# Three moves in the order of work: a difference of y, one gated product, and the differences of w_out

## The chip, the cores and the metric

The kernel runs on one core of one Trainium2 chip. The metric is the device time of one execution in microseconds (us), the median of three runs. PE is the matrix engine, DVE the vector engine, ACT the scalar engine, POOL the GpSimd engine and SP the engine whose queue issues most DMAs. PSUM is the memory that PE writes its products to, SBUF the memory for everything else on the core.

## The reference

Two blocks follow one another. The first is a chunked state space scan (batch 4, 8 heads, 768 positions, head size 32, state size 16); its output `y` becomes a matrix of 3072 tokens by 256. The second is a feed-forward block:

```
h = x @ w_in            # 3072x256 @ 256x2048
g = h * np.cos(h)
return (g @ w_out)      # 3072x2048 @ 2048x256
```

The arrays `w_in` and `w_out` come as 64-bit floats; the kernel makes 32-bit floats of them on the core.

## The kernel before

**Steps.** The tokens are worked in six chunks (`NC = 6`, counted from 0) of 512: 128 positions of four sequences. A chunk has 16 steps (`NF = 16`); step `n` is step `f` of chunk `c`, with `c, f = divmod(n, 16)`. A step takes half a chunk (256 tokens, `u`) and two of the sixteen 128-wide tiles of the hidden size (the pair `j` of eight). It has these parts:

- `first(n)` (line 660): eight PE instructions give `hp`, 128 by 512 values in PSUM. Steps in a "run" (`sevens`: steps 9 to 13 of chunks 2, 3 and 4, and 13 of the last chunk's steps) use `first7` (line 760) instead. It makes the same block from seven smaller products, with differences of `w_in` (`wid`, made once by `differ_in`) and differences of `y` (`yd`, made for each chunk by `differ_y`, line 742, the tile called `m` in the profile). Its products are issued in the order 1, 6, 7, 5, 4, 3, 2; product 4 reads the fourth difference `d[:, 3]`.
- `wind_k` (ACT, line 667), `wind_w` (DVE, line 673) and `gate` (ACT, line 682) give the cosine of `hp`.
- `gated(n)` (DVE, line 687) multiplies: `gT = hp * cos`. It is the last reader of `hp[n]`, so it frees the PSUM bank that a later `first` writes; outside the runs two such banks take turns from step 4 on, so `first(n)` waits for `gated(n - 2)`. For steps of chunk 1 and later, `gated` also calls `differ(n)`, three POOL instructions (lines 712, 714, 715, tile `gd`).
- `second(n)`, issued two steps later (`LAG = 2`): in chunk 0 eight PE instructions (line 796) with rows of `w_out`; from chunk 1 on `seven(n)`, fourteen PE instructions (line 836) that read `gT`, `gd`, `w_out` and the differences of `w_out` (`wd`, in the profile the tile `words`).

**Weights.** Each weight matrix comes in eight pieces. `grade` takes a piece apart: ACT makes the absolute value of the high word (line 248) and scales the low word (line 246), POOL clamps (line 249). `join(which, i)` puts it together: a DVE shift and mask (line 261), a DVE combination with the sign (line 263) and a POOL add (line 271) that writes the finished piece. `piece` says which piece is joined in which step: step `n` joins piece `n // 2` of `w_out` if `n` is even, a piece of `w_in` if it is odd. Step 4 joins piece 2 of `w_out`, the piece that the second products of steps 4 and 5 read.

**Differences of w_out.** `differ_w(i, js)` (POOL, line 706) makes difference `i` of four for a range of pairs: `fore` is four pairs, `mid` two, `hind` two. `differ_at` says after which step. The first reader is `seven(16)`, issued in iteration 18; `mid` is read first by `seven(20)`, in iteration 22.

**Order.** The schedule is written by hand: an engine executes its instructions in the order in which the program issues them, and waits by semaphores. Steps 0 to 3 stand in `first_steps`; the loop starts at step `AHEAD = 4`. In an iteration the loop issues `first(n)`, `wind_k`, `wind_w`, the next `grade`, `gate`, the `join`, `gated(n)`, then work of the scan (`decays0`, a DVE scan `lam`, line 375, and `weigh0`, POOL line 381), then `differ_y`, the sums of finished outputs (POOL line 861), `differ_w`, and last `second(n - 2)`. `differ_y` is called in steps 4 to 7 of chunks 2, 3 and 4, one difference a step, on POOL, for the second half of the chunk. Difference 3 reads difference 2.

Of the kernel before, what the change touches and what calls it, by code (L numbers as in the profile page):

```python
# [25 lines left out]
def kernel(  # L26
# [13 lines left out]
    V, ACT, G, PE = nc.vector, nc.scalar, nc.gpsimd, nc.tensor  # L40
# [4 lines left out]
    NC = S // P  # L45
    DM, DF = moe_w_in.shape
    KT = DM // P
    NF = DF // P
# [204 lines left out]
        if later:  # L253
            return rest

    def join(which, i):


        parts = held.pop((which, i), ())
        for e, (high, bits, last) in enumerate(parts):  # L260
            V.tensor_scalar(out=bits, in0=bits, scalar1=3, scalar2=0x3FFFFFFF,  # L261
                            op0=ALU.logical_shift_left, op1=ALU.bitwise_and)
            V.scalar_tensor_tensor(out=bits, in0=high, scalar=0xC0000000, in1=bits,
                                   op0=ALU.bitwise_and, op1=ALU.bitwise_or)
            dst = kept(which, i)
            if len(parts) > 1:
                dst = dst[:, :, e * P:(e + 1) * P]
            else:
                bits, last = (ap.rearrange("p (k f) -> p k f", k=dst.shape[1])
                              for ap in (bits, last))  # L270
            G.tensor_tensor(out=dst.bitcast(U32), in0=bits, in1=last, op=ALU.add)
# [412 lines left out]
    def gated(n):  # L684
        cos = turns.pop(n)
        gT[n] = ffn.tile([P, TB], FP32, tag="gT", bufs=LAG + 1, name="gT")
        V.tensor_tensor(out=gT[n], in0=hp.pop(n), in1=cos, op=ALU.mult)  # L687
        gT[n] = gT[n].rearrange("p (q m) -> p q m", q=4)
        if NF <= n < NC * NF - 1:
            differ(n)  # L690
# [42 lines left out]
    def differ_y(c, i, eng, us=slice(0, 2)):  # L733

        if i == 0:
            yd[c] = ms[2].rearrange("p (i u m) -> p i u m", i=4, u=2)
        d = yd[c]
        y11, y12, y21, y22 = (yT[c][:, us, k, h * P:(h + 1) * P] for k in range(2)
                              for h in range(2))
        a_ = (y12, y22, y22, y21)[i]  # L740
        b_ = (y11, y12, d[:, 0, us], d[:, 2, us])[i]
        eng.tensor_tensor(out=d[:, i, us], in0=a_, in1=b_,  # L742
                          op=ALU.add if i in (1, 2) else ALU.subtract)
# [203 lines left out]
    def store_a(dst, src):  # L947
# [3 lines left out]

    piece = {n: ("in", (n + 3) // 2) if n % 2 else ("out", n // 2) for n in range(NF)}
    fore, mid, hind = slice(0, NJ // 2), slice(NJ // 2, 3 * NJ // 4), slice(3 * NJ // 4, NJ)
    differ_at = {NF - 2: [(0, fore), (1, fore)], NF - 1: [(2, fore), (3, fore)],
                 **{NF + i: [(i, mid)] for i in range(4)},
                 NF + 4: [(0, hind)], NF + 5: [(1, hind)], NF + 6: [(2, hind), (3, hind)]}


# [61 lines left out]
    AHEAD = 4  # L1020
# [83 lines left out]
    for n in range(AHEAD, NC * NF + LAG):  # L1104
        c, f = divmod(n, NF)
        if n < NC * NF:

            if c > 0 and f in (loads_of := (6, 7, 8, 9) if c == 1 else (0, 1, 2, 3)):
                load(c + 2, loads_of.index(f))
            if n in (NF - 4, NF - 3):  # L1110
                load_arow(n - NF + 8)
            if n == NF - 2:
                for k in (4, 5):
                    for s in range(2):
                        load_x(k, s)
            if n in (NF - 1, NF):
                load_along(2, (2 * (n == NF), 2 * (n == NF) + 1))
            for e, i in chunks_at(n, "along"):
                load_along(e + 1, (2 * i, 2 * i + 1))
            if n in sevens or n - 1 in sevens:  # L1120
                first_of_seven(n)
            else:
                first(n)
            if n not in sevens and n - 1 in sevens:
                wind(n - 1)
                gate(n - 1)
                gated(late.pop())
            closing = f == NF - 1 and 1 <= c < NC - 1
            take_y = finish2(c + 1) if closing else None
            if n not in sevens:  # L1130
                wind_k(n)
                wind_w(n)
            if closing:
                take_y(0)
            for e, s in chunks_at(n - 1, "turn"):
                turn2(e, s)
            for k in units_at(n, 2):
                turn_unit(k)
            if n + 1 in piece:
                rests_of.append(grade(*piece[n + 1], later=True))  # L1140
            if n not in sevens:
                gate(n)
            while len(rests_of) > (n == AHEAD):
                rest = rests_of.pop(0)
                if rest:
                    rest()
            joins = n in piece and piece[n] in held
            if joins:
                join(*piece[n])

            behind = [lambda at=at: decays2(*at) for at in decays_at(n)]
            behind += [lambda k=2 * c - 1 + i: add_state(k) for c, i in chunks_at(n, "state")]
            behind += [lambda c=c, b=2 * s + p: reaches(c, b) for c, s in chunks_at(n, "reach")
                       for p in range(2)]
            behind += [lambda at=at: turn_blocks(*at) for at in chunks_at(n, "turn")]
            behind += [lambda k=k, p=p: decays0(k, p) for k, at in unit_at.items()
                       for p in range(2) if at[0][p] == n]
            behind = [lambda k=2 * c + i, q=q: weights(k, q) for c, i in chunks_at(n, "weigh")
                      for q in range(2)] + behind
            behind = [lambda k=k: weights(k, 1) for k in units_at(n - 1, 3)] + behind  # L1160
            if not joins and behind:
                behind.pop(0)()
            if n + 1 in sevens or n in sevens:
                late.append(n)
            else:
                gated(n)
            if closing:
                take_y(1)
            if n == NF + 7:
                weigh0(5)  # L1170
            if add_s and (n == NF - 5 or units_at(n - 1, 4)):
                exchange = add_s()
                add_s = None
            if n == NF + 9:
                exchange()
            for do in behind:
                do()
            if n == runs[-1][0] - 2:
                for i in range(4):
                    differ_y(NC - 1, i, V)  # L1180
            if 2 <= c < NC - 1 and 4 <= f <= 7:
                differ_y(c, f - 4, G, slice(1, 2))
            if unsummed and (c > 1 or summed[0]):
                unsummed[0](range(summed[0], summed[0] + 1), G)
                summed[0] = (summed[0] + 1) % 4
                if summed[0] == 0:
                    unsummed.pop()
            elif n not in sevens and f not in ((10, 11, 12) if c == 1 else (10, 11)):
                for do in unsummed:
                    do()  # L1190
                unsummed.clear()
            for k, ((_, last_), *_) in unit_at.items():
                if last_ == n:
                    weigh0(k)
        for i, js in differ_at.get(n, ()):
            differ_w(i, js)
        for start, js in zip((2 * NF - 5, 3 * NF - 3, 4 * NF - 3),
                             (slice(1, 6), slice(0, 1), slice(6, NJ))):
            if start <= n < start + 4:
                differ_in(n - start, js)  # L1200
        if f == NF - 2 and 1 < c < NC - 1:
            open2(c + 1)
        if n == AHEAD + 1:
            second(AHEAD - LAG)
        if n >= LAG and n != AHEAD:
            second(n - LAG)
        for e, _ in chunks_at(n, "inner"):
            inner2(e)
        for k in units_at(n, 3):
            for t in range(2):  # L1210
                inner(k, t)
            if k == 3:
                at = [gs[k, s][:, 0, 2 * P:] for s in range(2)]
                sums(4, at, group)
                take_sums((4,), at)
            weights(k, 0)
        for k in units_at(n, 4):
            take_s, add_s = finish0(k)
            take_s()
        for k in units_at(n, 1):  # L1220
            reach_unit(k)
        if n == 2 * NF - 3:
            open2(2)
        for at, e in block_loads.items():
            if at == n:
                loading = load_blocks(e)
            if at <= n < at + 12:
                next(loading)
# [30 lines left out]
```

## Time and profile before

| what | value |
|---|---|
| median of 3 runs | 366.38 us (366.14 to 366.74) |
| the profiled execution | 365.9 us, of which the span from first to last instruction is 364.1 us |
| granted clock of PE | 0.999 |
| PE busy | 356.6 us, 98% of the span |
| DVE busy | 275.6 us, 76% |
| POOL busy | 238.5 us, 65% |
| ACT busy | 183.9 us, 51% |

A row of the timeline gives the start, the time from start to end, the engine, the line, the operation, what is written from what, shapes, and the number of merged instructions; a bracket tells the idle time before and what ended it. A busy PE can hide a wait, since ends of matmuls are modelled; the distance between the starts of like rows shows it. Instructions overlap a little: on DVE the next one starts some 0.08 us before the end of the one before.

### The profile page before, as it was taken

Reading aid. Unit: us, or ns where it says so; the run is one execution under the profiler, and the core shown is the slowest. Engines: PE = TensorE matmul, PEld = TensorE weight load, DVE = VectorE, ACT = ScalarE, POOL = GpSimd, SP = SyncE. Lnnn points to the kernel's source line nnn. Section 1 sums busy time; section 2 is a strip of 40 time slices with the busy share of each in tenths; the row PEclk is TensorE's granted clock in tenths of the full one; section 3 lists DMA queues with packets and bytes.
Section 4 is the critical chain, followed back from the end, with each engine's and each line's share of the span. In section 5 each row is a group of like instructions: output and inputs, shape, how many; then the busy total and the mean of one; then the engine's idle time right before and its main releaser. Section 6 shows DMA issues by size and latency. Waiting matters only on the chain.

```text
span 364.1 us, 10279 instructions
## 1 busy us (share of the span) xinstructions
PE 356.6 (98%) x4070; PEld 326.1 (90%) x4070; DVE 275.6 (76%) x504; ACT 183.9 (51%) x352; POOL 238.5 (65%) x387
## 2 busy tenths in 40 slices
PE   7999999999999999999999999999999999999995
PEld 4788888888999999999989998999999999999995
DVE  7789998588777977877766877775776775778774
ACT  3597766544455254634445543545453544454542
POOL 5567757579866885765775666686666565475562
PEclk9999999999999999999999999999999999999999
DMA  7996957692564447011328102110001001001001
GB/s 140 274 358 136 214 109 119 109 135 58 112 105 71 91 93 104 8 44 41 75 58 122 17 6 66 31 34 12 0 2 31 0 3 32 0 3 31 1 15 46
DMA packets 97328, 26.43 MB, mean 73 GB/s; under 512 B 87328, under 2 KB 93184, under 8 KB 97280
## 3 DMA queue, kind: packets, MB, share of 16 engines
q1 hardware_dynamic: 96032, 25.38, 34.0%
q8 instruction: 32, 0.52, 0.6%
q10 hardware_dynamic: 1248, 0.39, 0.5%
q14 instruction: 16, 0.13, 0.1%
HBM read 22.36 MB, written 3.34 MB: 71 GB/s over the span
## 4 chain that ended last, share of the span: by engine, by line
PE 80%; DVE 6%; POOL 5%; SPq 2%; issue 2%; ACT 2%; DMA 2%; POOLq 0%; ACTq 0%; DVEq 0%
PE o L836 30%; PE hp L660 25%; PE m L760 7%; PE hp L760 5%; PE o L796 5%; PE y L629 2%; POOL gd L712 1%; DMA bc<-in_B_dram 1%; DVE w L673 1%; POOL gd L714 1%; DVE mag L261 1%; PE y L477 1%; POOL m L742 1%; ACT k L667 1%; PE y L617 1%
## 5 line engine op out<-in xcount | busy, mean ns | idle before, releaser
L660 PE MATMUL hp<-yT,w_in 128*128 128x256 f32 x544 | 129.4, 382 | 0.3 <-DVE gT L687 0.3
L660 PEld LDWEIGHTS hp<-yT,w_in 128*128 128x128 f32 x544 | 99.1, 190 | 13.6 <-issue 1.0
L712 POOL TENSOR_TENSOR gd<-gT 128x256 f32<-128x256 f32 x79 | 59.8, 757 | 77.6 <-DVE gT L687 64.0
L682 ACT ACTIVATE w<-w,quarter 128x512 f32<-128x512 f32 x96 | 69.4, 723 | 63.4 <-DVE w L673 63.2
L673 DVE SCALAR_TENSOR_TENSOR w<-hp,k 128x512 f32<-128x512 f32 x96 | 65.9, 686 | 45.4 <-ACT k L667 45.1
L667 ACT ACTIVATE k<-hp 128x512 int32<-128x512 f32 x96 | 57.1, 595 | 71.4 <-PE hp L660 63.0
L687 DVE TENSOR_TENSOR gT<-hp,w 128x512 f32<-128x512 f32 x96 | 65.5, 683 | 12.0 <-ACT w L682 7.9
L836 PE MATMUL o<-words,gd 128*128 128x128 f32 x474 | 66.2, 276 | 0.1
L836 PEld LDWEIGHTS o<-words,gd 128*128 128x128 f32 x474 | 59.4, 192 | 0.3 <-POOL gd L714 0.3
L836 PE MATMUL o<-w_out,gT 128*128 128x128 f32 x316 | 50.3, 278 | 0.0
L836 PEld LDWEIGHTS o<-w_out,gT 128*128 128x128 f32 x316 | 45.3, 191 | 3.1
L714 POOL TENSOR_TENSOR gd<-gT,gd 128x128 f32<-128x128 f32 x79 | 40.3, 510 | 6.2
L715 POOL TENSOR_TENSOR gd<-gT,gd 128x128 f32<-128x128 f32 x79 | 37.2, 471 | 6.2
L836 PE MATMUL o<-w_out,gd 128*128 128x128 f32 x158 | 30.7, 276 | 0.0
L375 DVE TENSOR_TENSOR_SCAN lam<-arow,unit 128x512 f32<-128x512 f32 x20 | 30.7, 1535 | 0.0
L836 PE MATMUL o<-words,gT 128*128 128x128 f32 x158 | 30.5, 275 | 0.0
L796 PE MATMUL o<-w_out,gT 128*128 128x256 f32 x128 | 29.9, 379 | 0.0
L796 PEld LDWEIGHTS o<-w_out,gT 128*128 128x128 f32 x128 | 24.2, 190 | 3.2
L836 PEld LDWEIGHTS o<-w_out,gd 128*128 128x128 f32 x158 | 24.0, 192 | 0.0
L836 PEld LDWEIGHTS o<-words,gT 128*128 128x128 f32 x158 | 24.0, 192 | 0.0
L760 PE MATMUL m<-m,wid 128*128 128x128 f32 x168 | 23.5, 276 | 0.0
L773 DVE TENSOR_TENSOR m<-m 128x128 f32<-128x128 f32 x28 | 8.2, 292 | 19.2 <-PE m L760 15.2
(130 smaller groups left out, 472.3 us busy)
## 6 DMA issues: line engine op xcount, KB each, us to landing
words<-in_moe_w_in_dram SPq DMA_DIRECT2D x8, 512.0 KB
words<-in_moe_w_out_dram SPq DMA_DIRECT2D x8, 512.0 KB
xr<-in_x_dram SPq DMA_DIRECT2D x24, 128.0 KB
arow<-a_cut SPq DMA_DIRECT2D x10, 256.0 KB
arow<-a_cut SPq DMA_DIRECT2D x10, 252.0 KB
out_dram<-sum SPq DMA_DIRECT2D x18, 128.0 KB
bc<-in_B_dram SPq DMA_DIRECT2D x24, 64.0 KB
blocks<-in_B_dram SPq DMA_DIRECT2D x16, 32.0 KB
```

The lines of the kernel that those rows point to most:

```text
L375: V.tensor_tensor_scan(out=lams[k][:, p, hs].rearrange(flat), data0=rows_.rearrange(flat), data1=unit0[:, hs].rearrange(flat), initial=0.0 ...
L660: PE.matmul(to_[:, e], lhsT=w_in[:, k, fs], rhs=y[:, k], start=(k == 0), stop=(k == KT - 1), skip_group_check=True)
L667: ACT.activation(k, hp[n], AF.Copy, bias=0.25, scale=INV_2PI)
L673: V.scalar_tensor_tensor(out=w, in0=hp[n], scalar=INV_2PI, in1=k, op0=ALU.mult, op1=ALU.subtract)
L682: ACT.activation(cos, cos, AF.Sin, bias=quarter, scale=TWO_PI)
L687: V.tensor_tensor(out=gT[n], in0=hp.pop(n), in1=cos, op=ALU.mult)
L712: G.tensor_tensor(out=d[:, 0:2], in0=g[:, 1:2].to_broadcast([P, 2, P]), in1=g[:, 3::-3], op=ALU.subtract)
L714: G.tensor_tensor(out=d[:, 2], in0=g[:, 0], in1=d[:, 0], op=ALU.subtract)
L715: G.tensor_tensor(out=d[:, 3], in0=g[:, 2], in1=d[:, 2], op=ALU.subtract)
L760: PE.matmul(dst[q], lhsT=w[q], rhs=y_[q], start=(q in (6, 1, 7)), stop=True, skip_group_check=True)
L796: PE.matmul(o[c, u][:, t], lhsT=g[:, 2 * e + t], rhs=w_out[:, 2 * j + e], start=(j == e == t == 0), stop=(j == NJ - 1 and e == 1), skip_gr ...
L836: PE.matmul(at[q], lhsT=a_[q], rhs=w[q], start=(j == 0 and q in starts), stop=(j == NJ - 1), skip_group_check=True)
```

## The change

Three things move; no instruction is added or left out, and no DMA is issued elsewhere.

1. The fourth difference of `y` (difference 3) is made in step 6 of chunks 2, 3 and 4, right behind the third, and no longer in step 7.
2. In step 4 the multiplication `gated(4)` is issued between the two DVE operations of the join of `w_out` piece 2, and no longer after both.
3. The differences of `w_out` start at step 13 instead of 14: the four `fore` ones in steps 13, 14, 14, 15 (before 14, 14, 15, 15), the four `mid` ones in steps 15, 16, 16, 17 (before 16, 17, 18, 19). The `hind` ones stay.

```diff
-    def join(which, i):
+    def join(which, i, between=None):
...
             V.tensor_scalar(out=bits, in0=bits, scalar1=3, scalar2=0x3FFFFFFF,
                             op0=ALU.logical_shift_left, op1=ALU.bitwise_and)
+            if between:
+                between()
             V.scalar_tensor_tensor(out=bits, in0=high, scalar=0xC0000000, in1=bits,
                                    op0=ALU.bitwise_and, op1=ALU.bitwise_or)
...
-    differ_at = {NF - 2: [(0, fore), (1, fore)], NF - 1: [(2, fore), (3, fore)],
-                 **{NF + i: [(i, mid)] for i in range(4)},
+    differ_at = {NF - 3: [(0, fore)], NF - 2: [(1, fore), (2, fore)],
+                 NF - 1: [(3, fore), (0, mid)], NF: [(1, mid), (2, mid)], NF + 1: [(3, mid)],
                  NF + 4: [(0, hind)], NF + 5: [(1, hind)], NF + 6: [(2, hind), (3, hind)]}
...
             if joins:
-                join(*piece[n])
+                join(*piece[n], (lambda: gated(n)) if n == AHEAD else None)
...
             if n + 1 in sevens or n in sevens:
                 late.append(n)
-            else:
+            elif n > AHEAD:
                 gated(n)
...
-            if 2 <= c < NC - 1 and 4 <= f <= 7:
-                differ_y(c, f - 4, G, slice(1, 2))
+            for i, at in enumerate((4, 5, 6, 6) if 2 <= c < NC - 1 else ()):
+                if at == f:
+                    differ_y(c, i, G, slice(1, 2))
```

## The prediction

> **What bounds the kernel now.** I read the page first, for the engine that is busy all the time and for the chain that ended last.
>
> ```profile
> PE 356.6 (98%) x4070; PEld 326.1 (90%) x4070; DVE 275.6 (76%) x504; ACT 183.9 (51%) x352; POOL 238.5 (65%) x387
> PE 80%; DVE 6%; POOL 5%; SPq 2%; issue 2%; ACT 2%; DMA 2%; POOLq 0%; ACTq 0%; DVEq 0%
> ```
>
> PE sets the time nearly everywhere. A change that adds no work and removes none can only pay where PE waits. So the second view is the list of waits, for PE alone:
>
> ```profile
> PE m L760 <- POOL m L742: 1.1, 2, 0.6
> PE hp L660 <- DVE gT L687: 0.3, 1, 0.3
> ```
>
> Two waits for a difference of `y` (line 742), together 1.1 us, and one of 0.3 us for a `gT`. The third view is the timeline around each, engine by engine. First the wait in chunk 2 (PE, POOL, DVE rows), and below it the same PE rows of chunk 4, which has no such wait:
>
> ```profile
> 165.21 0.83 PE L760 MATMUL m<-m,wid 128*128 128x128 f32 x6
> 166.60 0.49 PE L760 MATMUL m<-m,w_in 128*128 128x128 f32 x2 [0.55 <-POOL m L742]
> 161.88 0.46 POOL L742 TENSOR_TENSOR m<-yT,m 128x128 f32<-128x128 f32 x1
> 165.17 1.37 POOL L742 TENSOR_TENSOR m<-yT,m 128x128 f32<-128x128 f32 x1
> 164.92 1.37 DVE L375 TENSOR_TENSOR_SCAN lam<-arow,unit 128x512 f32<-128x512 f32 x1
> ...
> 280.47 0.83 PE L760 MATMUL m<-m,wid 128*128 128x128 f32 x6
> 281.14 0.39 PE L760 MATMUL m<-m,w_in 128*128 128x128 f32 x2
> ```
>
> The reader should see two things. Product 4 starts 1.39 us after the row before it in chunk 2 and 0.67 us after it in chunk 4. And the fourth difference took 1.37 us in chunk 2, while the third took 0.46: POOL's instruction lay beside the DVE scan `lam` (164.92 to 166.29) and ended 0.25 us after it. Chunk 3 shows the same at 222.9 (1.37 us).
>
> Now the start of the loop, around `gT` of step 4:
>
> ```profile
> 32.81 0.76 DVE L263 SCALAR_TENSOR_TENSOR mag<-words,mag 128x512 uint32<-128x512 uint32 x1
> 33.36 0.69 POOL L249 TENSOR_SCALAR mag<-mag 128x512 f32<-128x512 f32 x1
> 33.50 0.68 DVE L687 TENSOR_TENSOR gT<-hp,w 128x512 f32<-128x512 f32 x1
> 34.02 1.27 POOL L271 TENSOR_TENSOR w_out<-mag,last 128x512 uint32<-128x512 uint32 x1
> 34.33 1.97 PE L660 MATMUL hp<-yT,w_in 128*128 128x256 f32 x8 [0.34 <-DVE gT L687]
> 35.60 0.98 DVE L263 SCALAR_TENSOR_TENSOR mag<-words,mag 128x512 uint32<-128x512 uint32 x1
> 37.85 1.89 PE L660 MATMUL hp<-yT,w_in 128*128 128x256 f32 x8
> ```
>
> `first(6)` (34.33) waits for the bank that `gT` of step 4 frees at 34.18. Last, the place of the differences of `w_out`:
>
> ```profile
> 67.83 1.28 POOL L271 TENSOR_TENSOR w_out<-mag,last 128x512 uint32<-128x512 uint32 x1 [4.12 <-DVE mag L263]
> 73.84 2.62 POOL L706 TENSOR_TENSOR words<-w_out,words 128x512 f32<-128x512 f32 x2
> 75.36 2.18 DVE L375 TENSOR_TENSOR_SCAN lam<-arow,unit 128x512 f32<-128x512 f32 x1
> 88.03 0.45 POOL L714 TENSOR_TENSOR gd<-gT,gd 128x128 f32<-128x128 f32 x1
> 88.53 0.94 PE L836 MATMUL o<-words,gd 128*128 128x128 f32 x6
> ```
>
> POOL is idle for 4.12 us before 67.83. From there to 88.5 it is busy but for 1.74 us before 78.21, and PE, in the second product of step 18, starts its six `gd` products at 88.53, 0.73 us after the four before them, where the step before shows 0.45 (84.50 to 84.95). So PE waits 0.28 us for `gd`.
>
> **Part 1, the fourth difference in step 6.** One POOL instruction moves in each of chunks 2, 3 and 4. Its input is the third difference, done at 162.34. POOL is then idle until 163.41, when `gd` of step 7 starts (it waits for `gT` at 163.27). The moved instruction takes 0.46 us (the median of its line) and ends near 162.8: the idle time covers it, no scan runs then, and `gd` of step 7 is not late. If that cover were gone it would cost POOL 0.46 us, and PE nothing, since `gd` of step 7 is needed first at 167.8. What PE gains I take from the step's length: in chunk 2 the first products of step 9 go from 164.99 to 167.37, 2.38 us; in chunk 3 from 222.69 to 225.06, 2.37; in chunk 4 from 280.25 to 281.81, 1.56. Gain 0.82 and 0.81, together 1.63 us. Chunk 4 gains nothing; its fourth difference was in time at 280.89. Next behind the wait are the DVE sums of step 9: they stand behind `lam` on DVE, done at 166.29, and want product 4, then near 166.3; so no new wait. From 167.5 on PE runs without a wait of that size to the end, so the gain reaches the end. Bounds: 1.63 gained, or 0.8 if one of the two places finds another wait.
>
> **Part 2, gT of step 4 inside the join.** The cosine is ready at 32.52 (31.80 + 0.72) and the first half of the join ends at 32.78, so `gT` can run from 32.81 to 33.49 instead of 33.50 to 34.18. PE's sixteen products before `first(6)` start at 30.37 and take 0.216 us each, so `first(6)` could start at 33.82 and the next second product at 35.55, where it now starts at 36.13: 0.58 us. But three instructions queue behind. The second half of the join (line 263) starts at about 33.42 instead of 32.81. POOL's clamp (line 249) starts at 33.36 whatever DVE does. Whenever line 263 finds a POOL instruction running it ends 0.53 us after that one (the row at 35.60: 36.58, the clamp at 35.26 ending at 36.05). So it ends at 33.97 + 0.53 = 34.50 and not at 33.57, and POOL's add of piece 2 runs from 34.55 to 35.8 instead of 34.02 to 35.29. The second product of step 4 reads this piece: PE, ready at 35.55, starts near 35.9. Of the 0.58 us, 0.2 is left. The next join (step 5) waits for this add in its first half (it ended at 35.57, 0.28 after the add; now 36.1) and for a clamp in its second; it ends at 37.05 instead of 36.58, and `gT` of step 5 at 37.7 instead of 37.19. `first(7)` needs that bank: it starts near 37.85, where it starts now. So nothing is left at step 7. DVE has hardly any idle time from there to 54 us (rows of 0.2), so it stays 0.4 late; `first(11)` at 51.67 has `gT` of step 9 ready at 51.27, and the way from a `gT` to PE takes 0.15, so 0.25 of cover: PE loses 0.1 to 0.2. Bounds: 0.58 gained (line 263 gets in ahead of the clamp each time) and 0.3 lost. I take 0.1 lost, as the row at 35.60 shows the collision where the same two instructions meet.
>
> On the pair of DVE and POOL the Trainium skill (SBUF — State Buffer, "Who interferes with whom") says that a DVE instruction with two SBUF inputs and a GpSimd instruction that reads SBUF exclude each other, and that the later one blocks fully. It speaks against this part: `gT` reads `hp` from PSUM, so the clamp gets in during it. By the rule line 263 would need its whole 0.69 us after the clamp and end at 34.66, and part 2 would lose 0.25; the rows show 0.53 us, and I go by them.
>
> **Part 3, the differences of w_out.** Six POOL instructions move forward. The first `fore` one (1.25 us) goes to step 13, into the 4.12 us of idle time: free. Step 14 keeps two. In step 15 a `mid` one (0.73) replaces a `fore` one, so POOL is clear 0.6 us sooner than 76.46. The scan `lam` of step 16 waits for just that (it starts at 75.36 and ends at 77.54, 1.08 after POOL), and `gT` and `gd` of step 16 come 0.6 us sooner. But step 16 now gets two `mid` ones instead of one, and step 17 still one: ahead of `gd` of step 18 there is 0.73 us more, less the 0.6. That leaves it 0.1 us later, and PE's wait of 0.28 grows to about 0.4. Where a `gd` meets a scan it takes 1.64 instead of 0.73 (86.30), so where the scans fall can shift it by most of a microsecond, though most of this is already paid. After step 18, two `mid` ones fewer: `gd` of step 19 is 0.7 sooner, and PE did not wait for it. Bounds: 0.28 gained (the wait goes) and 0.4 lost; I take 0.1 lost, by the count of instructions.
>
> **Sum.** −1.63 + 0.1 + 0.1 = −1.4 us. The profiled execution took 365.9 us (span 364.1), so it would take 364.5; the median of the runs lies 0.5 above it at 366.38, so the predicted median is 365.0 us. Best: −1.63 − 0.58 − 0.28 = −2.5, 363.9 us. Worst of the bounds with part 1 whole: −1.63 + 0.3 + 0.4 = −0.9, 365.5 us.
>
> **Rivals.**
> - *All three waits go.* Speaking for it: each row has a visible wait, and 33.36 against 33.42 is a close race. Against it: the collision at the next join is there either way. 363.9 to 364.3 us.
> - *Collisions eat most of it.* Where a DVE instruction and a POOL one meet, rows lose 0.3 (line 263) to 0.9 us (`gd`, scans). Two such on PE's path in parts 2 and 3 leave −0.7 to 0: 365.7 to 366.4 us. Against it: PE has 0.25 to 1.2 us of cover at most steps.
> - *The wait for the fourth difference is replaced.* If product 4 finds another input late, or the DVE sums after it do, part 1 gives nothing: 366.4 to 366.6. Chunk 4 speaks against it, though it has no scan at that point.
> - *DVE's delay in steps 5 to 12 grows (the other side).* DVE is full there; scans there take 1.92 instead of 1.21 when they meet a POOL add. Late by 0.4 at step 7 with 0.25 of cover at step 11, each further meeting costs PE 0.7. From 1.6 us lost the change isn't faster, from 2.4 it is slower; three such meetings give 367.2. Against it: these scans meet the adds already.
>
> **How the numbers follow.** A difference under 0.2%, 0.73 us, can't be told from none. Forecast 60%, all waits gone 18%, collisions 12% (a quarter of it still beyond 0.73 us), part 1 replaced 5% (most of it within), DVE's delay 5%. Faster 0.81, same 0.13, slower 0.06. The range goes from the best, 363.9, to 366.1: the worst bound 365.5, the 0.36 by which the highest run lay above the median, and half of the collision case.
>
> **What would show it.** Part 1: the wait of PE for line 742 is gone, the fourth difference takes 0.46 us, and step 9 takes 1.56 us in chunks 2 and 3. Part 2: `first(6)` starts near 33.8, but the second product of step 4 only near 35.9, and `first(7)` near 37.85. Part 3: the scan of step 16 ends near 77, and PE still waits at step 18. The prediction is wrong if the step lengths in chunks 2 and 3 stay over 2 us, or if PE comes to 92 us more than half a microsecond away from where it came before.

## The result and the profile after

The changed kernel took 365.51 us (median of 16 runs), the kernel before 366.49 us beside it. The ratio is 0.9963, with a 95% interval of 0.9947 to 0.9979: 1.4 us faster, 0.8 to 1.9. The ratio is that of the means (366.76 and 365.40 us, 1.36 apart). The two medians lie only 0.98 us apart: five of the 16 runs of the kernel before took more than 367 us, one of the changed kernel, and a mean counts such runs while a median does not.

The profiled execution took 365.45 us with a span of 363.7 us, only 0.4 us under the span before. The spans hide most of the gain, since the way to the loop took longer in this execution: the product of step 4 starts at 27.78, before at 26.84. In the thirteen profiles of this study (both kernels and eleven experiments) it starts between 26.29 and 27.78, whatever the kernel. So below I count from the product of step 4 to the end of the span: 337.26 us before, 335.92 after, 1.34 less. That agrees with the ratio. Spans are printed to a tenth, so a distance to the end is good to about 0.1 us.

Line numbers are higher by 2 behind the changed function: line 660 is now 662, 760 is 762, 742 is 744, 263 is 265, 271 is 273.

The list of waits, PE alone, kernel after:

```profile
PE warm L84 <- PEq L1246: 0.8, 1, 0.8
PE y L517 <- issue: 0.7, 1, 0.7
PE g L458 <- ACT cT L401: 0.5, 1, 0.5
PE tp L397 <- POOL c L348: 0.3, 1, 0.3
```

The two waits for a difference of `y` are gone, and so is the one for a `gT`. Those that are left lie before step 4. The timeline around step 9 of chunk 2 (PE, POOL and DVE rows, kernel after):

```profile
166.48 0.39 PE L762 MATMUL hp<-yT,w_in 128*128 128x128 f32 x2
166.70 0.83 PE L762 MATMUL m<-m,wid 128*128 128x128 f32 x6
167.37 0.39 PE L762 MATMUL m<-m,w_in 128*128 128x128 f32 x2
168.04 0.61 PE L838 MATMUL o<-w_out,gT 128*128 128x128 f32 x4
163.37 0.99 POOL L744 TENSOR_TENSOR m<-yT,m 128x128 f32<-128x128 f32 x2
166.41 1.37 DVE L377 TENSOR_TENSOR_SCAN lam<-arow,unit 128x512 f32<-128x512 f32 x1
```

Product 4 (167.37) follows 0.67 us after the row before it, 1.39 before the change. The step takes 1.56 us (166.48 to 168.04). The third and the fourth difference are one merged row, 0.99 us for both, over at 164.36, before the scan starts at 166.41. Beside the scan there is now no POOL instruction that PE waits for.

Now the start of the loop, around `gT` of step 4 (kernel after):

```profile
33.52 0.46 POOL L947 TENSOR_SCALAR la<-a_in 96x256 f32<-96x256 f32 x1
33.65 0.68 DVE L689 TENSOR_TENSOR gT<-hp,w 128x512 f32<-128x512 f32 x1
34.25 0.68 DVE L265 SCALAR_TENSOR_TENSOR mag<-words,mag 128x512 uint32<-128x512 uint32 x1
34.31 1.08 POOL L249 TENSOR_SCALAR mag<-mag 128x512 f32<-128x512 f32 x1
34.76 1.89 PE L662 MATMUL hp<-yT,w_in 128*128 128x256 f32 x8
35.37 1.27 POOL L273 TENSOR_TENSOR w_out<-mag,last 128x512 uint32<-128x512 uint32 x1
35.45 1.47 DVE L261 TENSOR_SCALAR mag<-mag 128x512 uint32<-128x512 uint32 x1
36.69 1.99 PE L798 MATMUL o<-w_out,gT 128*128 128x256 f32 x8
38.59 1.99 PE L662 MATMUL hp<-yT,w_in 128*128 128x256 f32 x8
51.95 0.68 DVE L689 TENSOR_TENSOR gT<-hp,w 128x512 f32<-128x512 f32 x1
52.77 1.97 PE L662 MATMUL hp<-yT,w_in 128*128 128x256 f32 x8
```

The row at 33.52 is POOL's clipping of the input `a`, which stands ahead of the clamp in its queue. Counted from step 4's product, `first(6)` (34.76) comes 0.51 us sooner than before, the second product of step 4 (36.69) 0.38, `first(7)` (38.59) 0.20. The gain shrinks from row to row. The second half of the join (34.25) runs in 0.68 us and is not held up. It is the clamp (34.31) that has to wait and takes 1.08 us, 0.69 before; the add of piece 2 stands behind the clamp in POOL's queue and starts at 35.37, 7.59 us after step 4's product, where it was 7.18. The first half of the next join (35.45) waits for this add and takes 1.47 us, 0.87 before, and DVE does not make it good: `gT` of step 9 starts at 51.95, 24.17 us after step 4's product, where it was 23.75. `first(11)` (52.77) waits for the bank of this `gT` and comes 0.16 us later than before: here the gain has become a loss.

### The profile page after: what moved, and what is told of

It reads as the page before. It is cut to its first block, busy times and chain, and to the rows that moved or that the text cites. A ratio compares the mean times of both kernels' runs of the same rounds, so it can differ in the third digit from the quotient of the medians.

```text
span 363.7 us, 10280 instructions
## 1 busy us (share of the span) xinstructions
PE 357.1 (98%) x4070; PEld 326.1 (90%) x4070; DVE 275.4 (76%) x504; ACT 184.2 (51%) x352; POOL 237.5 (65%) x387
## 4 chain that ended last, share of the span: by engine, by line
PE 92%; POOL 3%; DMA 2%; DVE 1%; issue 1%; ACT 0%; POOLq 0%; DVEq 0%; ACTq 0%
PE o L838 34%; PE hp L662 31%; PE m L762 7%; PE o L798 7%; PE hp L762 5%; DMA bc<-in_C_dram 2%; PE y L631 2%; PE g L605 1%; PE y L479 1%; PE y L619 1%; POOL gd L714 1%; PE g L458 1%; POOL words L708 1%; PE y L527 1%; PE y L517 1%
## 5 line engine op out<-in xcount | busy, mean ns | idle before, releaser
L714 POOL TENSOR_TENSOR gd<-gT 128x256 f32<-128x256 f32 x79 | 58.9, 745 | 76.4 <-DVE gT L689 64.2
L377 DVE TENSOR_TENSOR_SCAN lam<-arow,unit 128x512 f32<-128x512 f32 x20 | 29.6, 1480 | 0.0
L762 PE MATMUL hp<-yT,w_in 128*128 128x128 f32 x112 | 21.6, 275 | 0.0
```

What stands on the lines that cost most here:

```text
L377: V.tensor_tensor_scan(out=lams[k][:, p, hs].rearrange(flat), data0=rows_.rearrange(flat), data1=unit0[:, hs].rearrange(flat), initial=0.0 ...
L714: G.tensor_tensor(out=d[:, 0:2], in0=g[:, 1:2].to_broadcast([P, 2, P]), in1=g[:, 3::-3], op=ALU.subtract)
L762: PE.matmul(dst[q], lhsT=w[q], rhs=y_[q], start=(q in (6, 1, 7)), stop=True, skip_group_check=True)
```

## The experiments

All rows of this table are differences to the kernel before, in us, counted from the product of step 4 in one profiled execution each; minus is sooner. Each column but the last is the start of a row of PE: `first(6)` the first product of step 6, "gd of step 18" its six products with `gd`, and so on. The last column is the distance to the end of the span. The kernel before, too, stands here with one execution, and differences of 0.2 us appear where nothing was changed: part 1 alone is 0.20 us sooner at step 6, long before part 1 acts.

| kernel | first(6) | first(7) | second(9) | first(15) | gd of step 18 | first(23) | step 9 of chunk 2 | step 9 of chunk 3 | end |
|---|---|---|---|---|---|---|---|---|---|
| the change | −0.51 | −0.20 | +0.24 | +0.46 | +0.41 | +0.37 | +0.55 | −0.40 | −1.34 |
| part 1 alone | −0.20 | −0.19 | −0.19 | +0.02 | +0.03 | −0.10 | +1.09 | +0.24 | −0.55 |
| part 2 alone | −0.50 | −0.19 | +0.26 | +0.41 | +0.42 | +0.42 | +0.66 | +0.53 | +0.61 |
| part 3 alone | +0.02 | +0.03 | +0.03 | +0.04 | +0.21 | +0.08 | +0.34 | +0.20 | +0.05 |
| parts 1 and 3 | +0.01 | +0.02 | +0.01 | +0.01 | +0.17 | +0.04 | +0.15 | −0.80 | −1.80 |
| part 2, clamp first | −0.51 | −0.18 | +0.25 | +0.50 | +0.44 | +0.43 | +0.45 | +0.32 | +0.38 |
| clamp first alone | +0.21 | +0.22 | +0.22 | +0.46 | +0.41 | +0.29 | +1.83 | +1.86 | +1.86 |
| fore differences alone | +0.02 | +0.03 | +0.02 | +0.28 | −0.02 | −0.25 | +0.44 | +0.39 | +0.17 |
| part 2, add first | −0.50 | −0.55 | +0.03 | +0.17 | +0.17 | +0.14 | +0.18 | +0.17 | +0.24 |
| part 1 and fore | 0.00 | +0.01 | 0.00 | +0.22 | −0.08 | −0.31 | +0.02 | −0.94 | −1.97 |
| the same, x later | −0.01 | 0.00 | 0.00 | +0.09 | −0.21 | −0.44 | −0.37 | −1.23 | −2.06 |
| part 1, part 2 with clamp first, fore | −0.50 | −0.17 | +0.28 | +0.70 | +0.41 | +0.18 | +2.57 | +1.61 | +0.62 |

The theory was that of the prediction: part 1 brings all, parts 2 and 3 cost a little. The rival was that part 2 keeps its half microsecond and something else takes it back.

### Part 1 alone

```diff
-            if 2 <= c < NC - 1 and 4 <= f <= 7:
-                differ_y(c, f - 4, G, slice(1, 2))
+            for i, at in enumerate((4, 5, 6, 6) if 2 <= c < NC - 1 else ()):
+                if at == f:
+                    differ_y(c, i, G, slice(1, 2))
```

> Part 1 alone (fourth difference of y in step 6). My theory: the two waits of PE at product 4 (step 9 of chunks 2 and 3) go and nothing takes their place; those steps take 1.56 us instead of 2.38 and 2.37, so the distance from the product of step 4 to the end of the span falls from 337.26 to about 335.6 us, and the time by 1.6 us (ratio 0.9956). Rival (the gain is partly paid back behind the waits): under 1.0 us, and a new wait in steps 10 to 13 of these chunks.

Measured: ratio 0.9952 (0.9938 to 0.9965), median 364.25 us, 1.8 us faster. In the profile both steps gained 0.81 us, as in every kernel with part 1. The distance to the end, though, is only 0.55 us shorter, because this one execution lost 1.15 us elsewhere, at step 25: PE waited for an operand of chunk 2's scan whose blocks landed late. This execution was the slowest of the six, 365.78 us; the other five took 364.13 to 364.47. DVE row and PE row of this kernel:

```profile
106.26 0.63 DVE L582 STREAM_TRANSPOSE turned<-blocks 128x256 f32<-128x256 f32 x1 [2.07 <-DMA blocks<-in_C_dram]
107.89 1.14 PE L603 MATMUL g<-cT,turned 32*64 32x128 f32 x56 [0.78 <-ACT cT L591]
```

The place has nothing to do with part 1, which acts 55 us later, and the kernels with the same wait below do not have part 1 in common. So a single profile can be wrong by a microsecond here; the table has to be read column by column, and the ratios decide on the whole.

### Part 2 alone

The change of `join` itself is that of the diff above; besides:

```diff
-                join(*piece[n])
+                join(*piece[n], (lambda: gated(n)) if n == AHEAD else None)
...
-            else:
+            elif n > AHEAD:
                 gated(n)
```

> Part 2 alone (gT of step 4 inside the join). My theory: the first product of step 6 comes 0.5 us sooner, counted from that of step 4, but the clamp of POOL gets in, the join ends later, and by the product of step 11 PE is 0.1 to 0.3 us later than before; the distance from step 4 to the end grows by 0.1 to 0.5 us. Rival (the delay seen with all three parts comes from something else, such as DMAs or the start): the 0.5 us stay, the distance falls by 0.3 to 0.5 us.

Measured: ratio 1.0005 (0.9996 to 1.0014): no gain, at most 0.15 us, and perhaps half a microsecond lost. The profile follows the changed kernel to a few hundredths: 0.50 us ahead at `first(6)`, 0.19 at `first(7)`, 0.26 behind at the second product of step 9. The rival, that the half microsecond stays, falls. The further 0.15 us at `first(15)` are not part 2's: part 1 alone has it too (from −0.19 to +0.02), and parts 1 and 3 together do not.

### Part 3 alone, and parts 1 and 3

Part 3 alone changes the table `differ_at` as the diff above has it; the other kernel adds part 1's edit.

> Part 3 alone (differences of w_out from step 13). My theory: up to step 13 nothing changes; at step 18 PE waits for gd about as long as before (0.28 us, to within 0.3), so the distance from step 4 to the end changes by -0.1 to +0.3 us. Rival (the backlog of POOL was the cause of this wait, and it goes): 0.28 us less. Other rival: the moved differences cause the 0.2 us that the changed kernel lost at the product of step 15; then that loss shows here too.

Measured: ratio 1.0002 (0.9989 to 1.0014), no difference. At step 18 PE's wait for `gd` grows by 0.18 us. This profile shows it as a wait (PE rows, and POOL's `gd` that ends it):

```profile
87.28 0.61 PE L836 MATMUL o<-w_out,gT 128*128 128x128 f32 x4
88.19 0.94 PE L836 MATMUL o<-words,gd 128*128 128x128 f32 x6 [0.29 <-POOL gd L714]
87.67 0.46 POOL L714 TENSOR_TENSOR gd<-gT,gd 128x128 f32<-128x128 f32 x1
```

0.91 us lie between the two PE rows, 0.73 before the change, 0.45 without a wait. By step 23 some of it is given back (+0.08). There is no loss at step 15, so the second rival falls. The first falls too: with this move the wait does not go.

> Parts 1 and 3, without part 2. My theory (part 2 costs a little): the distance from step 4 to the end is 0.1 to 0.5 us under that of the full change (335.92), about 335.6 us, and the time 1.5 to 1.7 us under the kernel before. Rival (part 2 gains): it is over that of the full change, 336.2 us or more.

Measured: ratio 0.9955 (0.9940 to 0.9970), median 364.16 us, and 1.80 us less to the end: part 1's 1.63; 0.14 us between step 9 of chunk 2 and step 9 of chunk 3; and some 0.17 us behind 323 us, where two PE rows are longer in the profile of before (0.92 and 0.47 us instead of 0.83 and 0.39, no wait shown) than in this one and in that of the full change; less the 0.15 us by which PE is late at step 9 of chunk 2. What the 0.14 and the 0.17 come from was not tried. Without part 2 the distance is some 0.4 us shorter than with it, as the theory had it.

### Why part 2 loses

The prediction had POOL's clamp slip in ahead of the second half of the join. If so, an earlier clamp should mend it.

```diff
-        clip_all()
...
-    for k in (2, 3):
-        G.memset(alongs[k][:, :, 0:1], 0.0)
-    rest_of_loads()
...
                 rests_of.append(grade(*piece[n + 1], later=True))
+            if n == AHEAD:
+                clip_all()
+                for k in (2, 3):
+                    G.memset(alongs[k][:, :, 0:1], 0.0)
+                rest_of_loads()
```

(Part 2's edit comes on top. `rest_of_loads` issues DMAs, which move along.)

> Part 2 alone, and POOL's clamp of step 4 issued ahead of the clipping of a and of three memsets, so that it is over before the second half of the join starts. My theory (part 2 loses since this clamp gets in ahead of the second half): the second half then ends 0.4 us sooner than with part 2 alone, the second product of step 4 doesn't wait for piece 2, step 7 keeps 0.3 to 0.5 us of the gain, and the bank of step 9 leaves 0 to 0.25 us of it at step 11, against 0.25 lost with part 2 alone. Rival (the join is late whatever the clamp does): as with part 2 alone, 0.2 us gained at step 7 and 0.2 lost at step 11.

Measured: ratio 1.0009 (0.9991 to 1.0026); on PE as with part 2 alone. My theory missed and the rival was right on the numbers. The profile shows why (DVE and POOL rows):

```profile
33.93 0.67 DVE L265 SCALAR_TENSOR_TENSOR mag<-words,mag 128x512 uint32<-128x512 uint32 x1
33.96 0.91 POOL L947 TENSOR_SCALAR la<-a_in 96x256 f32<-96x256 f32 x1
35.06 1.27 POOL L273 TENSOR_TENSOR w_out<-mag,last 128x512 uint32<-128x512 uint32 x1
```

The clamp was done in time, but now the clipping of `a` stood in its place: it met the second half of the join, took 0.91 us, and the add started 7.60 us after step 4's product, as before the mending.

The same move of the clamp, without part 2:

> The kernel before with only POOL's clamp of step 4 moved ahead of the clipping and the memsets. My theory: without part 2 no clamp is in the way of that join, so steps 6 and 7 start within 0.15 us of where they did, counted from step 4; later DMAs of a (stored after the clipping, 0.6 us later) change nothing on PE. Rival: the clamp's place matters by itself, and step 7 moves by more than 0.2 us.

Measured: ratio 1.0005 (0.9976 to 1.0033), steps 6 and 7 0.21 us late, a miss against my 0.15; the rival's 0.2 was nearer. The earlier clamp meets the second half of that join, which then takes 0.98 us instead of 0.76. (Here too the last block of chunk 2 was late, DVE waited 2.40 us for it, and PE lost 1.5 at step 25.)

So a new theory: what matters is not which of the two goes first, but that a POOL instruction that reads SBUF stands between the join's second half and POOL's add. With the clamp first and the clipping behind the add, nothing does (part 2's `join` line as above; `clip_all()` and the other lines are taken out where they stood, as above):

```diff
                 join(*piece[n], (lambda: gated(n)) if n == AHEAD else None)
+            if n == AHEAD:
+                clip_all()
+                for k in (2, 3):
+                    G.memset(alongs[k][:, :, 0:1], 0.0)
+                rest_of_loads()
```

> Part 2 alone, with POOL's clamp of step 4 ahead of the join and the clipping of a and the memsets behind POOL's add of piece 2, so that POOL has nothing between the second half of the join and the add. New theory, after the clamp moved by itself changed nothing: the add is late because one POOL instruction that reads SBUF stands between, whichever; it started 7.59 us after step 4's product with part 2, 7.18 before. It should now start near 7.2, the second product of step 4 come 0.5 us sooner than before, step 7 keep 0.4 to 0.5, and step 11 keep 0.1 to 0.3 us of gain instead of 0.2 lost. Rival (DVE itself is late by the moved gT, POOL's order is no matter): step 7 0.2 us sooner, step 11 0.2 us later than before, as with part 2 alone.

```profile
33.17 0.68 DVE L265 SCALAR_TENSOR_TENSOR mag<-words,mag 128x512 uint32<-128x512 uint32 x1
34.00 1.27 POOL L273 TENSOR_TENSOR w_out<-mag,last 128x512 uint32<-128x512 uint32 x1 [0.87 <-DVE mag L265]
35.41 1.91 PE L798 MATMUL o<-w_out,gT 128*128 128x256 f32 x8
37.16 1.89 PE L662 MATMUL hp<-yT,w_in 128*128 128x256 f32 x8
36.80 1.27 POOL L273 TENSOR_TENSOR w_in<-mag,last 128x512 uint32<-128x512 uint32 x1
37.50 0.85 DVE L261 TENSOR_SCALAR mag<-mag 128x512 uint32<-128x512 uint32 x1
50.66 0.68 DVE L689 TENSOR_TENSOR gT<-hp,w 128x512 f32<-128x512 f32 x1
```

The add starts 7.30 us after step 4's product (26.70 in this profile) and POOL waits for DVE, not the other way round. The second product of step 4 (35.41) comes 0.58 us sooner than before and `first(7)` (37.16) 0.55: the whole of what a free `gT` can bring. That shows the mechanism at steps 4 to 7: it is what stands between the join and the add on POOL. But the gain isn't kept. `gT` of step 9 (50.66) comes 23.96 us after step 4's product; before it was 23.75. On the way the first half of step 6's join (37.50) waits for POOL's add of step 5's piece and takes 0.85 us instead of 0.48. That add (36.80) starts 10.10 us after step 4's product, 9.89 before: the clipping, the memsets and the clamp of step 5 now stand ahead of it in POOL's queue. DVE, with under 0.4 us of idle time between steps 4 and 9, doesn't make it good. `first(11)` needs the bank of that `gT`, and behind it PE stands where it stood before (+0.03). Ratio 1.0011 (0.9994 to 1.0027). I had expected 0.1 to 0.3 us to be kept there, and that missed: the late add has moved on by one step. With `gT` of step 9 where it was before, about 0.25 us could have been kept at `first(11)` (the cover that the prediction worked out). Whether another place for the clipping would do that was not tried.

### The differences of w_out, fore alone

```diff
-    differ_at = {NF - 2: [(0, fore), (1, fore)], NF - 1: [(2, fore), (3, fore)],
+    differ_at = {NF - 3: [(0, fore)], NF - 2: [(1, fore), (2, fore)], NF - 1: [(3, fore)],
                  **{NF + i: [(i, mid)] for i in range(4)},
```

> Only the four fore differences of w_out begin a step sooner (13, 14, 14, 15); the mid ones stay in steps 16 to 19. My theory (part 3 costs 0.17 us at step 18 since a mid difference more stands ahead of gd): POOL is clear near 75.2 instead of 76.5, the scan of step 16 ends near 76.3, gd of step 16 starts near 77.0 instead of 78.2, and the wait of 0.28 us at step 18 goes, so that PE comes to step 21 0.2 to 0.3 us sooner than before. Rival (the place of the scans decides, not the count of POOL instructions): the wait at step 18 stays at 0.2 to 0.5 us.

```profile
75.77 1.21 DVE L375 TENSOR_TENSOR_SCAN lam<-arow,unit 128x512 f32<-128x512 f32 x1
77.64 0.73 POOL L712 TENSOR_TENSOR gd<-gT 128x256 f32<-128x256 f32 x1 [2.31 <-DVE gT L687]
88.20 0.61 PE L836 MATMUL o<-w_out,gT 128*128 128x128 f32 x4
88.64 0.83 PE L836 MATMUL o<-words,gd 128*128 128x128 f32 x6
```

The scan of step 16 takes 1.21 us, as long as alone, instead of 2.18, and `gd` of step 16 starts 0.70 us sooner (I had expected 1.2). `gd` of step 18 is in time: 0.44 us between the two PE rows. The wait goes, 0.29 us, and 0.23 more by step 23. All four profiles with the `fore` differences alone show 0.44 or 0.45 us at this place, the nine others 0.68 to 0.91. PE comes to step 18 0.28 us later here, but that isn't why: with part 2 alone it comes 0.41 us later and still waits as before (0.75 us between the rows). So the order of POOL's work is what made PE wait, and the early `mid` differences gave the gain back. The rival's number (a wait of 0.2 to 0.5 us) missed, but the place of the scans is part of it: before the change the first `gd` instruction of step 18 met a scan and took 1.64 us, here it takes 0.73, and a `mid` difference ahead of it meets the scan and takes 1.65. The ratio is 0.9994 (0.9977 to 1.0011), too wide to show a third of a microsecond, and this profile then lost 0.6 us at step 25, where DVE waited 1.52 us for the last block.

### Put together

> Part 1, part 2 with the clamp first, and only the fore differences sooner. My theory: the sum, 1.63 + 0.1 + 0.28 us, distance from step 4 to the end near 335.2 us, 2 us under the kernel before and 0.7 under the changed one. Rival: PE, ahead of DVE by that much at step 11, meets the next late gT or gd, and it ends no better than part 1 alone (335.6 us).

This is part 1, part 2 with the clamp first, and the fore differences. Measured: ratio 0.9975 (0.9944 to 1.0005), median 364.73 us: no better than part 1 alone (0.9952), with an interval too wide to decide between the sum and the rival. Its profile lost more than 2 us at step 25, where DVE waited 2.31 us for the last block of chunk 2; before that, it had part 2's loss instead of the 0.1 us that the sum counted on (+0.28 at the second product of step 9). The profiled execution took 367.10 us and is one of four above 367 among twelve.

> Part 1, and of part 3 the fore differences alone; no part 2. My theory: the sum of 1.63 and 0.3 to 0.5 us, so 1.9 to 2.1 us less from step 4 to the end where the blocks of B and C of chunk 2 come in time; where the DMA of the last of them is late (step 25, seen as 0.6 to 2.4 us of DVE's wait in four profiles) that much of it goes. Rival (the gain at step 18 is always eaten by that DMA): no better than part 1 alone, ratio 0.995.

Measured: ratio 0.9943 (0.9924 to 0.9962), median 364.05 us beside 366.27: 2.1 us faster than before. To the end it is 1.97 us less. By its ratio that is the fastest kernel of the study, and it does without part 2 and without the early `mid` differences. Its interval overlaps those of part 1 alone and of the changed kernel.

```diff
-            if n == NF - 2:
-                for k in (4, 5):
-                    for s in range(2):
-                        load_x(k, s)
+            if n in (NF - 2, NF + 5):
+                for s in range(2):
+                    load_x(4 if n == NF - 2 else 5, s)
```

> As the run before, and two of the four loads of x for chunk 2 are issued in step 21 instead of 14, so that SP's queue comes to the blocks of B and C 1.3 us sooner. Theory (SP's queue, which issues without a break from 33 to 98 us, sets when the last block lands): DVE's wait for it in step 23 falls under 0.3 us, PE has no wait for the scan's operand before step 25, and the time is 0.3 to 1 us under that of the run before. Rival (the blocks land late for another reason): the wait stays in the range of 0.2 to 2.4 us and the times are equal.

Measured: no wait of DVE for a block in this profile and 2.06 us less to the end, but a ratio of 0.9946 (0.9924 to 0.9969), median 364.07: equal to the run before. So the forecast of the wait came true and that of the time did not. That the queue sets when the block lands fits the profile; that it costs time in most executions is not shown. One profile without a wait proves little, as parts 1 and 3 had none either.

## Why the prediction was right

The forecast was −1.4 us; the means give −1.36 and the profile −1.34, the medians −0.98 (365.51 us against a forecast of 365.0). Part 1 is right in its mechanism and size, and it is nearly the whole. That the sum is right to 0.1 us is partly luck. Part 2 cost 0.14 us more than forecast and part 3 0.15 less. And terms that the sum does not have nearly cancel in this profile: +0.22 us ahead of step 15, −0.04 by step 23, +0.18 by step 9 of chunk 2, −0.14 from there to step 9 of chunk 3, −0.13 behind it. The sum, term by term:

- **Part 1, −1.63.** Measured −0.82 and −0.81, in every kernel that has it, with the fourth difference in idle time and nothing late behind it. The step without the wait in chunk 4 was the right yardstick: the idle time shown in the list of waits (1.1 us) would have given half a microsecond too little. The rival "the wait is replaced" is refuted.
- **Part 2, +0.1.** Measured +0.24 to +0.28 behind step 11 in the four kernels where the clamp or the clipping stands ahead of the add, inside the bounds of −0.58 and +0.3, but over the value taken. The course was right in its turns, to 0.2 us: 0.5 us gained at step 6, 0.2 left where piece 2 is needed (0.38 measured), nothing left at step 7 (0.20 measured), a loss at step 11. What failed is the order in it. The prediction let the second half of the join start at 33.42, behind a clamp that starts at 33.36. In the time of the profile before, the clamp's row did start at 33.37, but the second half started at 33.31, won the close race, and the clamp waited. The add came 0.41 us late instead of 0.53, for another reason than the one given: it queues behind the clamp on POOL. From there on the delay goes as forecast: the next join waits for the late add, and DVE stays 0.4 us late up to step 9.
- **Part 3, +0.1.** Alone +0.17 at step 18, as forecast by counting the instructions ahead of `gd`; in the full change −0.05 there: 0.69 us lie between the two PE rows, 0.73 before. PE comes there 0.46 us later, but that alone does not shorten the wait, as part 2 alone shows (0.41 us later, 0.75 us between the rows). The scan of step 17, behind which `gd` of that step ends, took 1.42 us with part 3 alone and 1.22 in the full change; why they meet POOL's work differently was not tried. The costs of parts 2 and 3 did not add here; the sum treated them as if they did.
- **The rivals.** "All three waits go" came half true: the three waits are off the list, yet the time behind two of them was not gained. The growing delay of DVE stayed at a quarter of a microsecond.

The Trainium skill (SBUF — State Buffer, "Who interferes with whom") says that a DVE instruction with at most one SBUF input, outside its two-port modes, leaves GpSimd alone, and that the later of two that do exclude each other blocks fully. The rows agree on the first: `gT`, with one operand in PSUM, took 0.68 us beside a clipping that took 0.46 as before the change, when the second half of the join ran beside it and took 0.76. On the second they show a little less: the blocked clamp ended 0.46 us after DVE's instruction, of the 0.61 that it takes alone. And its remark that issue order decides who blocks fits what my replay got wrong. That part 2 lost about the 0.25 us that the prediction worked out for a blocked second half is chance: in the change that half was not blocked.

## What to carry to other kernels

Price a wait by the distance between like steps with and without it, not by the idle time that the list of waits shows. When an instruction is moved forward, look at what stands behind it on the other engine's queue too: the half microsecond of part 2 was spent by a POOL instruction that nobody had moved, and DVE, with hardly any idle time, carried the delay on. And move no more work forward than the idle time holds: the move of the `fore` differences gained 0.3 us where it filled a gap, and with the `mid` ones moved too it lost 0.2, since they added one instruction ahead of a due one.

## What the runs showed of the hardware that I had not expected

- The way to step 4 took 26.29 to 27.78 us in thirteen profiles, without a link to what was changed. In a kernel that is bound by PE afterwards, all of this goes into the time.
- In the profile of the kernel before SP's queue issues DMAs from 33 to 98 us, with one break of 3.1 us ahead of 46.56, which the expectation of the last run leaves out, and none above 0.5 us behind it. The last block of chunk 2 lands close to its use. DVE's wait for it ran from none to 2.40 us, and PE's loss at step 25 from none to more than 2 us. Why it differs between executions stays open.
- In ten of the thirteen profiles PE loses 0.1 to 0.25 us in the scan's block of small products ahead of step 15, with no wait shown: the block's last row takes 0.99 to 1.14 us there, and 0.90 to 0.92 in the other three, the kernel before among them. No part of the change decides it: part 1 alone has it, parts 1 and 3 together do not. Its cause was not tried.
